# Another order table for the same 1,927 operations of a fused attention and gated MLP kernel

## The chip, the cores and the metric

One Trainium2 chip, one of its cores. The time is device microseconds of one execution of the whole program, as the median of several runs; lower is better. The engines are TensorE (PE, with PEld for its weight loads), VectorE (DVE), ScalarE (ACT), GpSimd (POOL) and SyncE (SP), which here issues every DMA.

## The reference

Causal attention over 4 batches, 12 heads, 448 positions and head size 64, then a gated MLP (768 wide, 1,024 inside) with a spatial gate, all in fp32:

```
scores = q @ k.T / sqrt(64); scores = where(causal, scores, -1e9)
attn   = softmax(scores); x = concat_heads(attn @ v)          # 4 x 448 x 768
h = gelu_tanh(x @ w_in); u, v = h[..., :512], h[..., 512:]
v_n = layernorm(v) * g_ln
v_s = einsum('ts,bsd->btd', w_sg, v_n) + b_sg
out = x + (u * v_s) @ w_out
```

## The kernel before

The 48 heads are worked as 24 pairs, p = 0 to 23, six to a batch; after a batch's six pairs comes its MLP. The five engines run far apart: pairs of the next batch are worked while PE does the MLP of the last.

**A pair.** q and k are loaded (L630, three buffers), PE makes the scores in two groups (L639, S0 and S1, in four PSUM banks with the tag s). DVE takes the row maxima with the mask (L653, eight a pair). ACT takes the exponentials into the P tiles and sums them (L661, ten a pair). DVE sums and inverts (L671, L672), PE transposes the inverses (L675, into one of the score banks), DVE copies them (L676), and two small DMAs and one large one spread them over the partitions (L680 rd, L683 rb). The exponentials must be transposed. For pairs 0 to 7 PE does it (L708, tags tx and ty), and ACT or DVE evict the result into a B buffer (L715, L713). For pairs 8 to 23 DVE does it with two stream transposes (L696, here called the first and the second turn of a pair), both into the one buffer A, which four DMAs copy into B (L700, `B<-P`). B has two slots. So the first turn of pair p writes A only when the four copies of pair p-1 have landed. Then PE multiplies by v (L738, PV, tag o; v is loaded at L732), DVE scales (L766), the result goes to DRAM (L771) and is split into a high and a low half on ACT or POOL (L774 to L779).

**The MLP.** `group` (L796) is every matmul of it, in operations of three: v (four groups of rows), u (four), s (the spatial gate, four), o (six). Each group takes a bank with the tag m. `gelu2` (L804 to L809) alternates ACT and DVE; layernorm is L847 to L864, the gate L908 to L914, the end L927 (residual load), L939 (add), L943 and L947 (stores).

**The weights.** w_in and w_out come in pieces through SP (L564), and each passes ACT (L566), DVE (L568, L570) and POOL (L573, L574). w_sg is L549 to L552, g_ln and b_sg L590 to L597.

**What sets the order.** Nothing runs as it is written. Every piece is added to an `Order` object with its engine, a duration that the planner assumes, what it reads and what it writes: 1,927 operations, of which 551 are PE's, 538 DVE's, 417 ACT's, 245 SP's and 176 POOL's. The table `ORDER` (from L92) gives each its rank: `ORDER[k] = n` makes operation n number k. `plan` takes, over and over, the engine that is free first in its own model and gives it the ready operation of lowest rank. The sequence that comes out is the program: each engine works its part strictly in that order. PSUM's eight banks and the buffers with several slots are handed out in the same sequence, so the order also sets whose bank an operation inherits, and whom it waits for.

Of the kernel before, what the change touches and what calls it, by code (L numbers as in the profile page):

```python
# [92 lines left out]
    1, 2, 84, 12, 4, 3, 118, 18, 5, 128, 6, 0, 172, 7, 24, 8, 162, 9, 10, 348, 85, 13, 14, 86, 15, 87, 16, 89, 11,  # L93
    88, 216, 17, 19, 90, 95, 91, 93, 96, 92, 129, 30, 94, 97, 20, 98, 99, 21, 130, 101, 133, 103, 22, 131, 100,
    134, 260, 23, 110, 102, 132, 25, 112, 104, 140, 26, 36, 105, 111, 27, 106, 139, 349, 28, 114, 113, 137, 29,
    141, 135, 115, 107, 116, 138, 108, 142, 173, 136, 146, 42, 117, 31, 32, 144, 33, 145, 119, 148, 175, 350, 34,
    177, 143, 176, 353, 35, 147, 178, 356, 183, 174, 149, 37, 109, 38, 185, 156, 48, 39, 184, 120, 304, 181, 157,
    40, 179, 150, 43, 154, 44, 186, 217, 41, 180, 351, 151, 155, 152, 160, 189, 45, 54, 354, 121, 182, 352, 187,
    218, 161, 357, 219, 188, 355, 221, 122, 359, 220, 158, 191, 192, 225, 206, 190, 222, 200, 46, 159, 634, 49, 50,
    47, 223, 163, 227, 193, 224, 153, 201, 164, 51, 231, 60, 165, 228, 123, 358, 204, 229, 226, 194, 124, 166, 230,  # L100
    205, 198, 233, 250, 52, 232, 261, 56, 234, 53, 195, 55, 196, 262, 263, 235, 265, 199, 57, 66, 236, 244, 360,
    678, 125, 264, 202, 245, 269, 58, 237, 203, 270, 361, 248, 271, 266, 238, 207, 278, 267, 273, 126, 167, 272,
    208, 268, 168, 276, 209, 62, 277, 210, 305, 59, 239, 294, 280, 249, 275, 197, 274, 242, 240, 309, 279, 169,
    307, 61, 458, 310, 72, 170, 243, 308, 475, 67, 281, 288, 63, 315, 246, 127, 289, 282, 68, 459, 247, 64, 283,
    598, 476, 316, 284, 69, 317, 306, 65, 318, 211, 241, 286, 313, 213, 212, 311, 292, 287, 314, 78, 635, 214, 312,
    722, 320, 293, 319, 290, 171, 639, 637, 70, 321, 477, 291, 74, 460, 322, 285, 71, 638, 324, 73, 251, 640, 323,
    75, 646, 252, 215, 325, 645, 253, 76, 254, 295, 648, 338, 255, 647, 77, 330, 79, 256, 332, 331, 80, 326, 636,
    257, 333, 327, 328, 81, 679, 764, 259, 641, 258, 643, 642, 296, 683, 681, 649, 297, 644, 82, 610, 298, 651,
    684, 334, 83, 668, 652, 299, 478, 650, 329, 682, 335, 461, 300, 301, 653, 654, 336, 302, 689, 655, 680, 337,
    690, 303, 691, 656, 806, 685, 662, 692, 657, 479, 687, 658, 663, 686, 462, 688, 695, 693, 660, 339, 696, 697,  # L110
    694, 340, 661, 341, 698, 342, 666, 699, 712, 343, 664, 659, 667, 700, 723, 345, 344, 665, 701, 702, 347, 346,
    724, 725, 727, 726, 362, 765, 728, 368, 733, 729, 463, 374, 734, 731, 767, 380, 769, 735, 480, 730, 848, 736,
    768, 464, 386, 492, 770, 481, 392, 493, 737, 465, 398, 363, 404, 706, 364, 466, 482, 494, 703, 707, 365, 467,
    495, 369, 366, 483, 367, 732, 509, 375, 376, 410, 381, 370, 468, 496, 741, 738, 371, 526, 377, 739, 372, 742,
    527, 382, 740, 373, 748, 393, 669, 387, 378, 416, 399, 379, 670, 405, 388, 422, 400, 671, 389, 749, 672, 390,
    510, 754, 391, 411, 511, 406, 394, 383, 497, 412, 417, 384, 673, 385, 528, 743, 674, 498, 424, 704, 407, 428,
    423, 395, 512, 434, 408, 484, 705, 409, 751, 744, 775, 529, 401, 750, 396, 469, 499, 530, 777, 402, 753, 397,
    745, 710, 500, 485, 746, 531, 403, 711, 501, 708, 440, 429, 470, 486, 766, 502, 446, 471, 709, 452, 418, 776,
    472, 752, 807, 425, 435, 419, 473, 1066, 426, 713, 413, 778, 420, 771, 811, 427, 714, 503, 773, 809, 474, 715,
    772, 747, 716, 487, 536, 774, 781, 796, 504, 779, 430, 537, 414, 717, 513, 421, 538, 810, 718, 783, 415, 780,  # L120
    514, 546, 782, 488, 431, 539, 784, 448, 505, 817, 489, 547, 432, 453, 548, 506, 819, 490, 433, 790, 549, 507,
    491, 556, 441, 447, 557, 675, 558, 454, 515, 508, 791, 719, 559, 540, 455, 794, 532, 677, 785, 541, 676, 516,
    795, 566, 533, 793, 517, 567, 721, 812, 534, 792, 720, 550, 518, 818, 551, 535, 542, 456, 568, 519, 457, 820,
    560, 543, 786, 520, 436, 561, 544, 521, 449, 522, 442, 808, 787, 450, 545, 788, 451, 755, 523, 1108, 815, 756,
    524, 813, 757, 816, 758, 525, 824, 797, 822, 838, 814, 798, 759, 789, 552, 799, 562, 443, 760, 553, 800, 761,
    444, 445, 563, 821, 569, 880, 437, 554, 574, 762, 570, 825, 582, 564, 555, 826, 575, 565, 438, 823, 439, 590,
    832, 571, 576, 591, 827, 763, 572, 833, 577, 592, 573, 828, 578, 849, 834, 801, 579, 835, 829, 850, 803, 851,
    836, 853, 852, 804, 580, 837, 1067, 857, 859, 855, 830, 854, 583, 581, 1150, 861, 1069, 858, 860, 593, 802,
    1070, 584, 805, 866, 856, 862, 585, 1077, 1071, 599, 586, 863, 604, 1072, 587, 865, 600, 594, 1079, 1078, 605,
    595, 867, 831, 1068, 1080, 874, 864, 588, 1109, 1192, 868, 1075, 589, 596, 1073, 839, 1076, 1074, 840, 597,  # L130
    1082, 1113, 841, 875, 1081, 842, 1084, 601, 1083, 1098, 869, 1086, 1111, 876, 1085, 606, 1114, 877, 1112, 870,
    602, 1120, 843, 879, 611, 1119, 1087, 878, 607, 871, 1122, 603, 845, 844, 616, 608, 1121, 872, 847, 617, 846,
    609, 1088, 1110, 1089, 1090, 1151, 1234, 1117, 1115, 1118, 1152, 1153, 1155, 1126, 1116, 1124, 618, 1276, 1154,
    1123, 1157, 619, 1128, 1159, 1127, 612, 873, 1156, 1125, 1092, 613, 614, 622, 1160, 623, 1161, 1091, 1093, 624,
    1163, 625, 615, 1096, 1168, 626, 1162, 1129, 1097, 628, 620, 1166, 1095, 1158, 1130, 629, 1164, 1131, 1170,
    1094, 630, 1165, 1132, 1167, 890, 1169, 621, 907, 1171, 627, 891, 1172, 892, 1173, 1174, 631, 1193, 632, 633,
    1194, 1195, 1197, 1196, 881, 1494, 1199, 1198, 882, 1133, 883, 1134, 884, 1099, 1140, 1200, 1203, 1100, 1030,
    1201, 1101, 1135, 1209, 1207, 1102, 1205, 908, 1182, 1211, 885, 1204, 1042, 1103, 909, 887, 1136, 1202, 1206,
    910, 1137, 888, 1210, 911, 1208, 1138, 889, 1212, 1139, 893, 1213, 886, 894, 1175, 1235, 1104, 1236, 1239,
    1237, 1240, 912, 1536, 1241, 1243, 924, 1238, 1244, 925, 1242, 1214, 895, 1215, 1216, 926, 896, 927, 913, 897,  # L140
    928, 914, 898, 929, 915, 1176, 941, 930, 899, 942, 1245, 1177, 1251, 943, 1247, 1249, 944, 931, 1181, 1250,
    958, 900, 1253, 1180, 932, 968, 916, 1217, 1252, 959, 1246, 901, 933, 1178, 969, 1254, 917, 1179, 1248, 960,
    934, 978, 918, 1255, 961, 919, 902, 920, 962, 903, 921, 979, 904, 980, 935, 905, 936, 970, 937, 922, 906, 988,
    963, 1105, 938, 1141, 945, 923, 1218, 1142, 939, 1143, 1144, 946, 1106, 1183, 1224, 1219, 947, 1184, 1107,
    1185, 940, 948, 1186, 1220, 971, 1145, 1222, 949, 1187, 964, 972, 1266, 950, 1221, 973, 965, 1223, 998, 974,
    951, 1146, 989, 966, 975, 1188, 990, 952, 1147, 967, 991, 976, 953, 1149, 1189, 954, 992, 977, 1148, 999, 981,
    955, 982, 1190, 956, 993, 957, 1006, 1191, 1260, 983, 1007, 984, 1261, 1008, 994, 1000, 985, 1014, 1265, 995,
    1001, 986, 1264, 1009, 996, 1002, 1262, 1015, 987, 1003, 1263, 1016, 997, 1017, 1010, 1022, 1004, 1018, 1011,
    1256, 1277, 1257, 1258, 1005, 1012, 1278, 1279, 1281, 1280, 1495, 1578, 1013, 1282, 1287, 1285, 1225, 1288,
    1283, 1019, 1499, 1226, 1259, 1497, 1289, 1286, 1227, 1290, 1500, 1294, 1228, 1284, 1292, 1267, 1308, 1498,  # L150
    1506, 1268, 1229, 1269, 1291, 1230, 1293, 1270, 1295, 1496, 1508, 1526, 1302, 1296, 1020, 1537, 1231, 1620,
# [854 lines left out]
```

## Time and profile before

| | |
|---|---|
| median of 3 runs | 354.4 us (353.96 to 354.82) |
| the profiled execution's own time | 355.62 us |
| its span, first to last instruction | 353.8 us |
| mean granted TensorE clock | 0.998 |
| PE busy | 339.1 us, 96% of the span |
| PE's weight loads (PEld) | 269.2 us, 76% |
| DVE, ACT, POOL busy | 260.0 us (73%), 196.6 us (56%), 149.9 us (42%) |
| data moved | 69.50 MB, mean 196 GB/s |

A busy share is a mean over stages. PE stands still for some 15 us in all, so the places where it does are few and can be looked at one by one. Times inside the program are counted from the start of the span. The profiled execution is 1.2 us longer than the median of the runs.

### The profile page before, as it was taken

The numbers are of one execution on the slowest core, as the hardware profiler recorded it, in microseconds if no ns is written. First come the engines' busy times: TensorE is split into PE (matmuls) and PEld (weight loads), VectorE is DVE, ScalarE is ACT, GpSimd is POOL, SyncE is SP. The second block draws the span as 40 slices with busy tenths as digits, with TensorE's granted clock in tenths as the row PEclk, the third lists the DMA queues.
The fourth block names the chain that finished last, engine by engine and source line by source line (L and its number), as shares of the span: only waits on it lengthen the run. The fifth ranks groups of instructions, "written<-read, shape, count | busy, mean of one in ns | idle before, by whom it ended". The sixth has DMA issues, their size and how long they took to land.

```text
span 353.8 us, 6879 instructions
## 1 busy us (share of the span) xinstructions
PE 339.1 (96%) x2231; PEld 269.2 (76%) x2231; DVE 260.0 (73%) x762; ACT 196.6 (56%) x658; POOL 149.9 (42%) x200
## 2 busy tenths in 40 slices
PE   7698999989999999999999999998999999999995
PEld 3455667657888778776898888776898898889995
DVE  2999978689999988756899987377897721258613
ACT  2999987777856957237443885218344700135410
POOL 4567887236977720010653641001265700242550
PEclk9999999999999999999999999999999999999999
DMA  7988987697855887797575786889465455400004
GB/s 237 374 284 292 304 287 228 196 287 210 248 123 173 219 238 250 242 298 248 151 173 128 235 236 176 269 240 295 121 200 126 139 119 196 155 2 1 0 2 156
DMA packets 37972, 69.50 MB, mean 196 GB/s; under 512 B 3888, under 2 KB 18992, under 8 KB 37936
## 3 DMA queue, kind: packets, MB, share of 16 engines
q1 hardware_dynamic: 37936, 69.06, 64.2%
q8 instruction: 18, 0.29, 0.3%
q14 instruction: 18, 0.15, 0.1%
HBM read 39.68 MB, written 12.58 MB: 148 GB/s over the span
## 4 chain that ended last, share of the span: by engine, by line
PE 69%; DMA 13%; DVE 9%; ACT 4%; SPq 3%; issue 1%; POOL 1%; DVEq 0%; POOLq 0%
PE m L796 47%; PE o L738 10%; PE s L639 8%; DMA B<-P 5%; ACT P L661 3%; DVE s L653 3%; DVE P L696 2%; DMA vn<-in_w_in_dram 2%; DMA out_dram<-res 2%; DMA rb<-rd 2%; PE tx L708 1%; DMA g<-in_w_out_dram 1%; DMA res<-xd 1%; PE ty L708 1%; SPq L680 1%
## 5 line engine op out<-in xcount | busy, mean ns | idle before, releaser
L661 ACT ACTIVATE P<-s,ngm 64x64 f32<-64x64 f32 (+3 forms) x240 | 100.3, 432 | 38.6 <-DVE ngm L653 18.4
L653 DVE CUSTOM_DVE_ANT_0 s<-s,mask 128x192 f32<-128x192 f32 (+3 forms) x192 | 75.3, 444 | 5.8 <-PE s L639 5.8
L796 PE MATMUL m<-win,x 128*128 128x512 f32 (+1 forms) x264 | 67.1, 399 | 0.0
L796 PE MATMUL m<-x,win 128*128 128x448 f32 x288 | 64.1, 370 | 1.8 <-ACT P L661 1.1
L796 PE MATMUL m<-g,wout 128*128 128x448 f32 x288 | 62.1, 368 | 0.0
L796 PEld LDWEIGHTS m<-x,win 128*128 128x128 f32 x288 | 53.3, 188 | 8.4 <-ACT P L661 1.9
L796 PEld LDWEIGHTS m<-g,wout 128*128 128x128 f32 x288 | 53.4, 188 | 5.4 <-issue 0.2
L796 PEld LDWEIGHTS m<-win,x 128*128 128x128 f32 (+1 forms) x264 | 46.8, 183 | 12.5 <-ACT P L661 0.6
L639 PE MATMUL s<-qk 64*128 64x448 f32 (+3 forms) x384 | 53.5, 403 | 1.8 <-DMA qk<-in_qk_dram 1.7
L639 PEld LDWEIGHTS s<-qk 64*128 64x128 f32 (+1 forms) x384 | 33.6, 178 | 23.2 <-issue 13.2
L661 ACT ACTIVATION_READ_ACCUMULATOR P<-s,ngm 128x1 f32 (+1 forms) x240 | 49.6, 207 | 0.0
L738 PE MATMUL o<-B,vraw 128*64 128x64 f32 (+4 forms) x672 | 47.2, 292 | 2.0 <-ACT P L661 1.4
L777 POOL TENSOR_TENSOR x<-xt,x 128x448 fp32r<-128x448 f32 x24 | 27.8, 1162 | 46.1 <-ACT x L776 45.9
L696 DVE STREAM_TRANSPOSE P<-P 128x1024 f32<-128x1024 f32 x32 | 39.3, 1233 | 9.5 <-DMA B<-P 4.4
L738 PEld LDWEIGHTS o<-B,vraw 128*64 128x64 f32 x672 | 33.0, 137 | 15.9 <-issue 6.3
L796 PE MATMUL m<-wsg,vn 128*128 128x448 f32 x176 | 39.6, 369 | 0.0
L851 POOL TENSOR_TENSOR mv<-mv,mhalf 128x1 f32<-128x1 f32 (+1 forms) x16 | 9.4, 592 | 67.7 <-DVE mv L849 67.2
L796 PEld LDWEIGHTS m<-wsg,vn 128*128 128x128 f32 x176 | 32.7, 188 | 3.2 <-issue 0.2
L804 ACT ACTIVATE tmp<-m 128x448 f32<-128x448 f32 (+1 forms) x28 | 15.2, 565 | 22.7 <-PE m L796 21.1
L807 ACT ACTIVATE tmp<-tmp 128x448 f32<-128x448 f32 (+2 forms) x32 | 18.9, 603 | 14.4 <-DVE tmp L805 14.1
L653 DVE DVE_READ_ACCUMULATOR2_ANT ngm<- 128x1 f32 (+1 forms) x192 | 25.7, 134 | 0.0
L805 DVE SCALAR_TENSOR_TENSOR tmp<-tmp,m 128x448 f32<-128x448 f32 (+1 forms) x28 | 17.3, 633 | 11.2 <-ACT tmp L804 11.1
(77 smaller groups left out, 379.5 us busy)
## 6 DMA issues: line engine op xcount, KB each, us to landing
B<-P SPq DMA_DIRECT2D x64, 256.0 KB
qk<-in_qk_dram SPq DMA_DIRECT2D x24, 448.0 KB
vn<-in_w_in_dram SPq DMA_DIRECT2D x12, 512.0 KB
vraw<-in_vP_dram SPq DMA_DIRECT2D x24, 256.0 KB
rb<-rd SPq DMA_DIRECT2D x24, 256.0 KB
xd<-xt SPq DMA_DIRECT2D x24, 224.0 KB
res<-xd SPq DMA_DIRECT2D x9, 448.0 KB
out_dram<-res SPq DMA_DIRECT2D x9, 448.0 KB
```

What stands on the lines that cost most here:

```text
L639: nc.tensor.matmul(out=s[z][bk].t[0:w, col:col + n], lhsT=qk_.t.rearrange("p a s -> p (a s)")[r, q0:q0 + w], rhs=qk_.t[r, 1, 0:n], start=T ...
L653: nc.vector.tensor_tensor_reduce(out=o, in0=o, in1=mk, scale=-0.125, scalar=3e38, op0=ALU.add, op1=ALU.min, accum_out=ngm[ib[z]][c][0:m])
L661: act(n, lambda c=c, m=m, k0=k0, n=n, bk=bk, col=col, off=off, kc=kc, i=i, z=z: nc.scalar.activation(out=P[i][0:m, off:off + n], in_=s[z][ ...
L696: dve(PW, lambda z=z: nc.vector.transpose(A[ia][:, :, :, z, :].rearrange("p g t k -> p t g k"), P[ib[z]]), Pk[z] + [kp], Ak, Tt, 1.105)
L708: nc.tensor.transpose(out, P[ib[z]][:, col:col + 128], ident)
L738: nc.tensor.matmul(out=dst(o.t[r]), lhsT=vr.t[:, c, r], rhs=src(z), start=first and n == 0, stop=last and n == len(lst) - 1)
L777: pool_tt(S, lambda: nc.gpsimd.tensor_tensor(out=y.t[:, S + 64:], in0=x.t, in1=f(y.t)[:, 0:S], op=ALU.subtract), [x, y], [(y, 1)], Ty)
L796: nc.tensor.matmul(out=ps.t[0:l().shape[1], 0:n], lhsT=l(), rhs=rr(), start=(k == 0), stop=(k == len(mms) - 1))
L804: act(n, lambda: nc.scalar.activation(out=z(), in_=h(), func=AF.Square), [ps], [t], at)
L805: dve(n, lambda: nc.vector.scalar_tensor_tensor(out=z(), in0=z(), scalar=1.0 / GC, in1=h(), op0=ALU.add, op1=ALU.mult), [ps], [t], at)
L807: act(n, lambda: nc.scalar.activation(out=z(), in_=z(), func=AF.Tanh, scale=GS * GC), [], [t], at, True)
L851: od.add("pool", 0.46, lambda mv=mv, m=m: nc.gpsimd.tensor_tensor(out=mv.t[0:m, 1:2], in0=mv.t[0:m, 1:2], in1=mhalf[0:m], op=ALU.pow), ["s ...
```

## The change

Only the table `ORDER` is another. The operations, their number, shapes, buffers, slots and the planner are the same. The new table was searched with an objective of which three quarters take transfers to land late. Its first rows:

```
 ORDER = (
-    1, 2, 84, 12, 4, 3, 118, 18, 5, 128, 6, 0, 172, 7, 24, 8, 162, 9, 10, 348, 85, 13, 14, 86, 15, 87, 16, 89, 11,
...
+    2, 4, 84, 1, 12, 5, 18, 6, 3, 24, 7, 128, 8, 0, 172, 9, 118, 10, 162, 11, 348, 85, 13, 14, 86, 87, 89, 15, 19,
...
```

Three places show what it moves.

**DVE in the head of the program, around the first pair's inverse.** `vn` is a piece of w_in on its way through L568 and L570; ngm_101 to ngm_108 are row maxima of pair 1; `tot` and `rs` are the sum and the inverse of pair 0. Before:

```order
L653 ISA s,ngm_105<-s,mask 64x64
...
L653 ISA s,ngm_104<-s,mask 128x448
L653 ISA ngm_104 128x1
L568 TENSOR_SCALAR vn<-vn 128x512
L671 TENSOR_REDUCE tot<-sm_117 128x8
L672 RECIPROCAL rs<-tot 128x8
L570 SCALAR_TENSOR_TENSOR vn<-vn 128x512
```

and in the change:

```order
L568 TENSOR_SCALAR vn<-vn 128x512 x2
L570 SCALAR_TENSOR_TENSOR vn<-vn 128x512 x2
L653 ISA s,ngm_105<-s,mask 64x64
...
L653 ISA s,ngm_104<-s,mask 128x448
L653 ISA ngm_104 128x1
L671 TENSOR_REDUCE tot<-sm_117 128x8
L672 RECIPROCAL rs<-tot 128x8
```

Two w_in pieces, not one, now pass whole ahead of pair 1's maxima and of the inverse; before, the second stood around the inverse. In the same stretch SP issues two more w_in loads ahead of pair 1's q and k, and the first v load behind them. On PE all seven warming matmuls (L538) come ahead of pair 0's scores, where one of them stood behind.

**SP where w_out is loaded, at pair 7.** `g` is a piece of w_out, `rd_127<-rT_123` the inverses of pair 7. Before:

```order
L680 DMA rd_127<-rT_123 4x16x128 x2
L564 DMA g<-in_w_out_dram 128x384 x4
L630 DMA qk<-in_qk_dram 128x896
L564 DMA g<-in_w_out_dram 128x384 x4
L683 DMA rb<-rd_127 128x1x512
L564 DMA g<-in_w_out_dram 128x384 x3
```

and in the change:

```order
L630 DMA qk<-in_qk_dram 128x896
L564 DMA g<-in_w_out_dram 128x384 x7
L680 DMA rd_127<-rT_123 4x16x128 x2
L564 DMA g<-in_w_out_dram 128x384 x2
L683 DMA rb<-rd_127 128x1x512
```

Seven of the sixteen w_out pieces now stand ahead of the DMAs that wait for pair 7's inverses; before, all stood behind.

**DVE around pair 20's first turn.** `P_92<-P_90` is a turn of pair 20; ngm_101 to ngm_108 are row maxima of pair 21, ngm_93 to ngm_100 of pair 22. Before:

```order
L653 ISA s,ngm_106<-s,mask_83 128x192
L653 ISA ngm_106 128x1
L848 BN_AGGR mv<-st 128x2
L696 STREAM_TRANSPOSE P_92<-P_90 128x8x4x32
L849 TENSOR_SCALAR mv<-mv 128x1
L653 ISA s,ngm_103<-s,mask 128x320
L653 ISA ngm_103 128x1
L653 ISA s,ngm_98<-s,mask_83 128x192
```

and in the change:

```order
L653 ISA s,ngm_103<-s,mask 128x320
L653 ISA ngm_103 128x1
L653 ISA s,ngm_93<-s,mask 64x64
L653 ISA ngm_93 64x1
L653 ISA s,ngm_107<-s,mask 128x320
...
L848 BN_AGGR mv<-st 128x2
L696 STREAM_TRANSPOSE P_92<-P_90 128x8x4x32
L653 ISA s,ngm_96<-s,mask 128x448
L653 ISA ngm_96 128x1
```

The last maxima of pair 21 and the first two of pair 22 are moved ahead of the turn.

## Rows read from the trace of the kernel before

**Rows 1.** The page, busy time: us (share of the span) xinstructions.
```profile
PE 339.1 (96%) x2231; PEld 269.2 (76%) x2231; DVE 260.0 (73%) x762; ACT 196.6 (56%) x658; POOL 149.9 (42%) x200
```

**Rows 2.** Waits of PE: line <- releaser: us in total, times, longest.
```profile
PE s L675 <- DVE rs L672: 2.0, 1, 2.0
PE s L639 <- DMA qk<-in_qk_dram: 1.7, 1, 1.7
PE o L738 <- ACT P L661: 1.4, 1, 1.4
PE m L796 <- ACT P L661: 1.1, 1, 1.1
...
PE m L796 <- DVE tmp L809: 0.6, 1, 0.6
```

**Rows 3.** Windows in the head: stretch, length, PE, PEld, DVE, ACT, POOL, clock, DMA, GB/s.
```profile
8.00:10.20 2.20, 0.53 (x5) 0.10 (x1) 2.20 (x12) 1.15 (x3) 1.63 (x2) 1.00 1.01 402
...
26.00:38.00 12.00, 10.42 (x82) 6.83 (x80) 11.83 (x46) 11.91 (x44) 9.63 (x11) 1.00 0.89 309
```

**Rows 4.** The page's costliest group of DVE: forms xcount | busy, mean ns | idle before.
```profile
L653 DVE CUSTOM_DVE_ANT_0 s<-s,mask 128x192 f32<-128x192 f32 (+3 forms) x192 | 75.3, 444 | 5.8 <-PE s L639 5.8
```

**Rows 5.** Timeline of PE in the head: start, us, engine, line, operation [idle before].
```profile
4.79 3.41 PE L639 MATMUL s<-qk 64*128 64x448 f32 x16
...
10.22 2.06 PE L639 MATMUL s<-qk 64*128 64x448 f32 x16 [1.70 <-DMA qk<-in_qk_dram]
...
15.35 0.27 PE L675 MATMUL s<-ident,rs 128*8 128x128 f32 x1 [2.04 <-DVE rs L672]
```

**Rows 6.** The chain that ended last, in the head: start, us, what.
```profile
15.20 0.56 DVE vn L570
```

**Rows 7.** The same chain at pair 6's PV.
```profile
67.62 0.28 SPq L680
...
71.02 5.10 DMA g<-in_w_out_dram
...
76.52 1.15 ACT P L661 x6
77.72 1.96 PE o L738 x20
```

**Rows 8.** The same chain from pair 14's first turn to its PV.
```profile
156.16 7.00 DMA B<-P
163.29 1.25 DVE P L696
164.53 0.58 DVE tmp L809
165.16 8.38 PE m L796 x39
173.54 3.68 PE o L738 x64
```

**Rows 9.** The same chain at pair 20's first turn.
```profile
231.83 4.74 DMA B<-P
236.69 1.25 DVE P L696
...
244.78 2.18 PE m L796 x9
```

**Rows 10.** Timeline of DVE: second turns of pairs 11, 13, 17, 19; first of 18.
```profile
124.14 1.23 DVE L696 STREAM_TRANSPOSE P<-P 128x1024 f32<-128x1024 f32 x1
...
149.02 1.24 DVE L696 STREAM_TRANSPOSE P<-P 128x1024 f32<-128x1024 f32 x1
...
201.15 1.24 DVE L696 STREAM_TRANSPOSE P<-P 128x1024 f32<-128x1024 f32 x1
...
210.19 1.25 DVE L696 STREAM_TRANSPOSE P<-P 128x1024 f32<-128x1024 f32 x1 [0.20 <-DMA B<-P]
...
224.20 2.37 DVE L696 STREAM_TRANSPOSE P<-P 128x1024 f32<-128x1024 f32 x2 [1.85 <-DMA vraw<-in_vP_dram]
```

192 rows, old and new, of the table ORDER are left out of this document.

## The prediction

> **What bounds the kernel now.** I read the page's busy times first. PE works 339.1 of 353.8 us [rows 1]; the reader is to see that only the 14.7 us in which PE stands can be won by an order, because the change takes no instruction away. Part of it lies ahead of the first matmul and behind the last one. Next come the waits of PE, for the rest [rows 2]. Two lie in the head: 1.7 us on pair 1's q and k, 2.0 us on pair 0's inverse. Three lie later, one wait each: 1.4, 1.1 and 0.6 us. The windows of the head show why PE does not recover there: from 26 to 38 us it works 10.42 of 12 us while DVE works 11.83 and ACT 11.91 [rows 3]. So up to some 38 us DVE and ACT bound the kernel, and from there PE does, but for the three waits. The chain that ended last, read at these three places, tells where each comes from.
>
> - Pair 6's PV, 77.72. SP stood for pair 7's inverses until 67.62, the w_out pieces queued behind them; the piece issued at 71.02 landed 5.10 us later; ACT, which works in order, stood for it, did its step and only then, at 76.52, six exponentials of pair 8 [rows 7]. PV had inherited a score bank of pair 8.
> - Pair 14's first turn. The copies out of A landed 7.00 us after 156.16, the turn ran, and only then the L809 that frees a bank for the matmul at 165.16 [rows 8].
> - Pair 20's first turn. The copies issued at 231.83 landed 4.74 us later, and behind the turn stood the maxima of pairs 21 and 22 that the bank of the matmul at 244.78 waited for [rows 9].
>
> **The change part by part.** It removes and adds no instruction, so everything is position; PE's changes of tile shape number 81 in either order, hence nothing there.
>
> *The head.* With each operation at its duration in the trace (DVE's largest group is L653, 444 ns, [rows 4]) I added up, at each operation that PE waits for, what the other engine has to do until then, less what PE has to do. The largest excess is how far PE must fall behind. DVE: 6.0 us before (at pair 4's L675), 4.8 in the change. ACT: 4.9 before (at pair 2's PV), 4.2 in the change. That is a gain of 0.7 to 1.2; I take 1.0. The bounds: two w_in loads are issued ahead of pair 1's q and k and the first v load behind them, a net 256 KB, which at the 402 GB/s of that stretch [rows 3] delays these scores (at 10.22, [rows 5]) by 0.65 us; and one L570 of 0.56 us [rows 6] moves ahead of pair 0's inverse. Exposed in full they cost 1.2 with no gain. At the other end both waits of the head, 3.7 us together, could shrink by half, 2. I stay near the middle because DVE's work fills the time until q and k land.
>
> *Pair 6's PV.* Seven w_out pieces are issued ahead of the wait for pair 7's inverses, some 4 us of PE's work earlier, and by the banks that the new order hands out this PV follows its own eviction, not pair 8's exponentials. That eviction has 7.0 us of ACT's work ahead of it and 8.3 us of PE's: 1.3 us to spare. Gain 1.4. What is late next is that eviction; a late w_out piece in front of it could still cost up to the 1.4 again.
>
> *Pair 14's first turn.* In the change the matmul that needs a bank at this place waits for the copy L676 of pair 15, which comes directly behind the turn and has some 2 us to spare, so a wait as long as the one seen hides. Gain 0.6, at least 0.
>
> *Pair 20's first turn.* The last maxima of pair 21 and two of pair 22 stand ahead of the turn, and the bank at this place comes from a v group of the MLP. Gain 1.1, at least 0.
>
> *The tail.* The change ends with one split add and one other, as before with two; nothing, within 0.5.
>
> *New waits.* The A chain has less room in places, below. Nothing shows its cost; the bounds are 0 and the rival's 3.6. The two waits at turns that rows show cost 0.6 and 1.1 [rows 2]; I take one such, 0.9.
>
> Sum: -1.0 - 1.4 - 0.6 - 1.1 + 0.9 = -3.2. Against the profiled execution's 355.62 that is 352.4; the median of the runs, 354.4, stands 1.2 below it, so 351.2.
>
> **The rivals.**
>
> *A, slower: the A chain.* Each pair from 8 on needs A empty, and DVE stands at the first turn until the copies of the pair before have landed. From the end of a second turn to that landing, where DVE waited for it: 7.8 us from pair 17 to 18, 13.0 from 13 to 14, 10.1 from 19 to 20 [rows 8 to 10]. In the change less DVE work fills this time: 4.7 us ahead of pair 18 (6.6 before), 4.9 ahead of pair 19 (6.4). So DVE stands more, and PE pays where what follows has no room. The place that decides is pair 14's PV, four such links behind pair 11's second turn. In the trace of before 48.2 us lie between them (124.14 + 1.23 to 173.54, [rows 8, 10]); PE's work between them in the change is 45.4, of which three double turns with what is between them take 7.8: 37.6 us for four links, 9.4 each. Up to 9.4 nothing happens, and without new waits the sum gives 351.2 - 0.9 = 350.3. At 10.3, the mean of the three seen, it costs 4 x 0.9 = 3.6 and gives 353.9, no change. At 11 it costs 6.4 and gives 356.7, slower. It decides at 10.6 (4 x 1.2 = 4.8, and 355.1). For it speaks the 13.0. Against it: the three seen are those that DVE had to wait for, so the long ones, and before PE did not wait at this PV with 2.8 us more of room.
>
> *B, part of the gain: the head gives nothing.* If q and k and the L570 are exposed, the head costs 1.2 instead of winning 1.0: 351.2 + 2.2 = 353.4. The clock belongs here. In the trace PE stood 1.70 us ahead of 10.22 and the granted clock of that stretch was 1.00 [rows 3, 5]; the sixteen score matmuls of pair 0 before it took 3.41 us, those of pair 1 2.06. With all warming matmuls ahead and q and k later the gap would be some 2.7 us. If the clock fell to its lower level, 1.2 GHz, pair 1's scores would cost 3.41 - 2.06 = 1.35 us more and end 352.6, hidden in part under DVE's work. The Trainium skill, "TensorE: Matmul & The Clock Gate", Part 1, has the rule that speaks against this change: an array that stands idle falls back to half its rate and must earn the full one again. The trace shows no fall at the 1.70 us gap, so it neither bears the rule out nor refutes it for a longer one.
>
> *C, no change: waits change places.* With PE at 96% each stage hands its delay on; if three new waits like the old ones (1.4, 1.1, 0.6) come up and the head gives 0.5, the sum is -0.5: 353.9. For it speaks that several places in the new order have under 0.8 us to spare by the same sums: the last add of batch 0 behind pair 11's turns, pair 22's transposed inverse ahead of pair 23's, pair 19's copies, which wait for pair 17's PV to free a B slot.
>
> *D, the change does nothing*: if the sequence came out the same. It does not: the engines' orders differ from the first rows.
>
> On the price of a copy out of A the rows alone decide: 4.74 and 7.00 us [rows 8, 9]. The Trainium skill, "SBUF — State Buffer", The DMA setup-cost knee, gives a fit of 2 us plus the bytes over 436 GB/s; an estimate by that page is 2.6 us for 256 KB. By it rival A would be dead; the trace disagrees, so A keeps its chance.
>
> **How the numbers follow.** A measurement of this kernel can tell about 0.2%, 0.7 us, from no change. The forecast, with its new waits between 0 and 2, holds 0.58 (349.4 to 352.4); B 0.16 (352.4 to 353.7); C and A's mild form 0.12 (353.7 to 355.1); A's hard form 0.14 (above 355.1). Faster 0.74, same 0.12, slower 0.14. The low end of the range is all three waits gone, no new ones, and the head at 1.9: 354.4 - 3.1 - 1.9 = 349.4; the high end takes in C and part of A's mild form, 354.9. Some 0.05 is left below, 0.15 above.
>
> **What would show it.** Right: no wait of PE over 0.5 us at the places that stood at 77.72, 165.16 and 244.78; ACT without a wait of 1.7 us on w_out ahead of pair 6's PV; PE at pair 6's PV some 2 us earlier; DVE standing longer in sum at L696 for `B<-P`, yet PE's waits from 38 us on under 1.5 us in all. Wrong: PE waiting at a PV (L738) for `B<-P`, at pair 14 above all (A); pair 1's scores near 3.4 us, or L675 of pair 0 past 16 us without recovery (B); new waits of PE on ACT or DVE adding to 3 us (C).

## The result, and the profile after

The change takes 349.36 us (median of 4 runs, 348.67 to 350.23) against 354.42 of before: ratio 0.986, 95% interval 0.983 to 0.989. Forecast were 351.2 us and a gain of 3.2; measured is a gain of 5.1. The profiled execution took 349.76 us with a span of 347.9, so the two profiled executions lie 5.9 us apart, 0.8 more than the medians.

The page's busy times: PE has the work of [rows 1] in a span shorter by 5.9 us.

```profile
PE 338.4 (97%) x2231; PEld 269.2 (77%) x2231; DVE 259.1 (74%) x762; ACT 196.0 (56%) x658; POOL 150.0 (43%) x200
```

All waits of PE in the change (line <- releaser: us in total, times, longest):

```profile
PE s L639 <- DMA qk<-in_qk_dram: 2.8, 1, 2.8
PE m L538 <- DVE tmp L533: 1.5, 1, 1.5
PE m L796 <- ACT P L661: 0.5, 1, 0.5
PE tx L708 <- ACT P L661: 0.5, 1, 0.5
PE o L738 <- ACT B L715: 0.3, 1, 0.3
```

The three later waits of [rows 2] are gone; one new one of 0.5 us stands at 269.7. The wait on pair 0's inverse is gone too, that on pair 1's q and k grew from 1.7 to 2.8. The windows (stretch, length, busy time of PE, PEld, DVE, ACT, POOL, then clock, DMA share, GB/s) show two things: PE is full where it stood before, and the clock fell in the head.

```profile
10.00:13.00 3.00, 2.25 (x10) 1.34 (x12) 2.47 (x9) 3.00 (x16) 1.11 (x2) 0.61 1.03 366
13.00:16.00 3.00, 3.00 (x22) 2.19 (x20) 2.97 (x13) 2.52 (x11) 2.92 (x3) 0.82 0.88 309
66.00:80.00 14.00, 14.00 (x73) 11.29 (x73) 13.21 (x36) 11.49 (x33) 6.45 (x13) 1.00 0.70 227
150.00:166.00 16.00, 16.00 (x105) 12.46 (x104) 15.74 (x45) 10.31 (x33) 4.59 (x6) 1.00 0.89 273
236.00:246.00 10.00, 10.00 (x75) 8.34 (x72) 9.97 (x31) 6.96 (x24) 2.90 (x4) 1.00 0.54 127
246.00:300.00 54.00, 53.52 (x361) 45.89 (x360) 30.28 (x70) 18.45 (x54) 20.66 (x24) 1.00 0.61 168
```

PE's timeline in the head of the change, beside [rows 5]: after a gap of 2.84 us pair 1's scores take 3.67 us, where they took 2.06 behind a gap of 1.70. Ahead of pair 1's q and k SP issues three w_in loads in the change and two in before, so one more and not two; with the first v load moved behind them the net is the 256 KB that the forecast worked with.

```profile
4.55 3.36 PE L639 MATMUL s<-qk 64*128 64x448 f32 x16
10.75 3.67 PE L639 MATMUL s<-qk 64*128 64x448 f32 x16 [2.84 <-DMA qk<-in_qk_dram]
...
15.28 0.27 PE L675 MATMUL s<-ident,rs 128*8 128x128 f32 x1
```

**PE's lag.** The waits listed do not add up to the gain, so I worked out a second measure from the traces. For each PE operation: its start, less the sum of the durations of all operations ahead of it in PE's own order, each at the shorter of its two durations in the traces of before and of the change, idle time left out. What is left is what PE has lost up to there. The columns on the right are the experiments below; every column is the trace of one execution.

| PE work done, us | before | change | wout_loads | copies_first | cut_rev | cut_late | warm_again |
|---|---|---|---|---|---|---|---|
| 50 | 11.3 | 10.6 | 10.5 | 12.0 | 12.4 | 10.4 | 10.0 |
| 70 | 14.0 | 11.1 | 11.7 | 14.3 | 13.1 | 12.2 | 10.6 |
| 140 | 15.8 | 13.3 | 14.3 | 16.2 | 15.3 | 14.3 | 12.8 |
| 150 | 17.2 | 13.6 | 17.1 | 16.4 | 15.5 | 14.5 | 13.0 |
| 200 | 19.2 | 14.7 | 19.2 | 17.8 | 16.7 | 15.6 | 14.1 |
| 230 | 21.9 | 15.6 | 22.4 | 18.6 | 17.7 | 16.6 | 15.1 |
| 260 | 22.8 | 16.8 | 23.2 | 19.5 | 18.8 | 17.7 | 16.2 |
| 330 | 23.3 | 17.3 | 23.7 | 20.0 | 19.2 | 18.1 | 16.6 |

Against before, the change has won 0.7 us by 50 us of work, 2.9 by 70, 2.5 by 140, 3.7 by 150, 4.5 by 200, 6.3 by 230, 6.0 by 260 and 5.9 at the end.

The columns also show how far executions of one order lie apart. Up to some 47 us, before, wout_loads, copies_first, cut_rev and cut_late run the same operations in the same order; at 50 us of work they lie between 10.4 and 12.4. So a difference of under 2 us between two columns can be chance there. What is lost from 140 us of work to the end is steadier: some 7.4 us in before and 9.4 in wout_loads, which have the old order there, and 3.8 to 4.0 in the change, in cut_rev, cut_late and warm_again, and in copies_first.

### The profile page after: what moved, and what is told of

Read it like the earlier page. It is cut to its first block, busy times and chain, and to the rows that moved or that the text cites. A ratio compares the mean times of both kernels' runs of the same rounds, so it can differ in the third digit from the quotient of the medians.

```text
span 347.9 us, 6879 instructions
## 1 busy us (share of the span) xinstructions
PE 338.4 (97%) x2231; PEld 269.2 (77%) x2231; DVE 259.1 (74%) x762; ACT 196.0 (56%) x658; POOL 150.0 (43%) x200
## 4 chain that ended last, share of the span: by engine, by line
PE 85%; DVE 5%; ACT 5%; DMA 2%; issue 1%; SPq 0%; DVEq 0%
PE m L796 62%; PE s L639 10%; PE o L738 10%; ACT P L661 3%; DMA qk<-in_qk_dram 2%; DVE s L653 2%; PE tx L708 1%; PE ty L708 1%; DVE vn L568 1%; ACT vn L566 1%; DVE vn L570 1%; PE s L675 1%; ACT B L715 1%; DVE ngm L653 1%; ACT wsg L551 0%
## 5 line engine op out<-in xcount | busy, mean ns | idle before, releaser
L653 DVE CUSTOM_DVE_ANT_0 s<-s,mask 64x64 f32<-64x64 f32 (+3 forms) x192 | 75.5, 442 | 6.6 <-PE s L639 6.5
L796 PE MATMUL m<-x,win 128*128 128x448 f32 x288 | 63.3, 368 | 0.0
L796 PEld LDWEIGHTS m<-g,wout 128*128 128x128 f32 x288 | 53.4, 188 | 5.9 <-issue 0.2
L796 PEld LDWEIGHTS m<-win,x 128*128 128x128 f32 (+1 forms) x264 | 46.9, 183 | 12.2 <-issue 1.3
L639 PEld LDWEIGHTS s<-qk 64*128 64x128 f32 (+1 forms) x384 | 32.2, 183 | 24.0 <-issue 13.0
L738 PEld LDWEIGHTS o<-B,vraw 128*64 128x64 f32 x672 | 33.9, 137 | 15.6 <-issue 5.7
L796 PE MATMUL m<-wsg,vn 128*128 128x448 f32 x176 | 38.2, 367 | 0.5 <-ACT P L661 0.5
L776 ACT ACTIVATE x<-xt 128x448 fp32r<-128x448 f32 x18 | 10.4, 578 | 37.2 <-DVE xt L766 35.3
L912 POOL TENSOR_TENSOR tmp<-tmp,g 128x448 f32<-128x448 f32 x16 | 18.1, 1144 | 21.3 <-DVE tmp L908 21.2
L779 POOL TENSOR_TENSOR x<-xt,x 128x64 fp32r<-128x64 f32 x24 | 8.7, 362 | 40.8 <-ACT x L776 40.6
```

The costliest lines, as they stand in the source:

```text
L639: nc.tensor.matmul(out=s[z][bk].t[0:w, col:col + n], lhsT=qk_.t.rearrange("p a s -> p (a s)")[r, q0:q0 + w], rhs=qk_.t[r, 1, 0:n], start=T ...
L653: nc.vector.tensor_tensor_reduce(out=o, in0=o, in1=mk, scale=-0.125, scalar=3e38, op0=ALU.add, op1=ALU.min, accum_out=ngm[ib[z]][c][0:m])
L738: nc.tensor.matmul(out=dst(o.t[r]), lhsT=vr.t[:, c, r], rhs=src(z), start=first and n == 0, stop=last and n == len(lst) - 1)
L776: act(S, lambda: nc.scalar.activation(out=y.t[:, 0:S], in_=x.t, func=AF.Copy), [x], [y], Ty, True)
L779: pool_tt(64, lambda: nc.gpsimd.tensor_tensor(out=y.t[:, S:S + 64], in0=x.t[:, S - 64:], in1=f(y.t)[:, S - 64:S], op=ALU.subtract), [x, y] ...
L796: nc.tensor.matmul(out=ps.t[0:l().shape[1], 0:n], lhsT=l(), rhs=rr(), start=(k == 0), stop=(k == len(mms) - 1))
```

## The experiments

Two theories stood against each other. Theory 1, that of the forecast: each wait of PE is cured where it stood, and the gains add. Theory 2: behind 111 us the old order is held by the landing of the copies out of A, so what is won ahead of these places is lost again at them.

One expression is used in several kernels: the first K operations of one table's sequence, then the rest in the other's.

```
     def run(self):
-        for n in self.plan():
+        head, then = self.sequence(CHANGED)[:312], self.sequence(ORDER)
+        for n in head + [n for n in then if n not in set(head)]:
             self.ops[n]["fn"]()
```

Here `sequence(table)` ranks the operations by that table and returns `plan()`. CHANGED is the new table, ORDER the old one.

**The new head alone (cut_head), the edit above.** Expected:

> The first 312 operations (to about 47 us of PE's time) in the new sequence, the rest in the old one. By place (theory 1: each wait of PE is cured where it stood, and the gains add): the head is worth 0.9 us, so 353.5, with the waits of 1.4 us at pair 6's PV, 0.6 at a u matmul of batch 1 and 1.1 at one of batch 2 all still there. By handing on (theory 2: PE falls back on the next late operation, gains shrink behind the place): the gain of the head is eaten at pair 6's PV, which waits on an absolute time (the landing of a w_out piece): 354.2 to 354.6, with that wait grown to 2.3 us.

Measured: 355.02 us against 355.28 of before beside it, ratio 1.002 (0.998 to 1.006). The head alone is worth nothing that can be measured, as theory 2 has it in its result; theory 1's 0.9 us lies just outside the interval. In its detail neither is borne out: the wait at pair 6's PV did not grow to 2.3 us, it was absent, and three small ones of 1.5 us in all stood at transposes of other pairs, the two longest at 53.4 and 81.8 us (columns as above; the lines of the spliced kernels are 104 further down, L812 is L708). And PE's lag at 50 us of work is 11.6 here, 11.3 in before: in this execution the head had won no lead that could have been handed on.

```profile
PE tx L812 <- DVE xt L870: 1.5, 3, 0.7
...
PE m L900 <- ACT P L765: 1.1, 2, 0.7
```

**New up to 111 us (cut_wout): the same with 780 in place of 312.** Expected:

> The first 780 operations (to about 111 us) new, the rest old. Theory 1: head 0.9 plus pair 6's PV 1.7, so 351.8; the waits of 0.6 and 1.1 still there. Theory 2: 353.5 or more, since the A chain of pairs 11 to 14 sets its own time and the old order's wait behind pair 14's first turn grows from 0.6 by what was won.

Measured: 356.08, ratio 1.004 (1.000 to 1.007). The splice itself does harm: PE's lag, 11.5 at 100 us of work (before 14.9), is 15.6 at 120, since around pairs 10 to 13 the two orders differ in which operations have been done. It tells only that the lead was gone right behind the splice, not why; inconclusive between the theories.

**New up to 168 us (cut_b1): the same with 1112.** Expected:

> The first 1112 operations (to about 168 us) new, the rest old. Theory 1: 0.9 + 1.7 + 1.0 = 3.6, so 350.8, with one wait of 1.1 left behind pair 20's first turn. Theory 2: under 2.5 in all, with that wait grown past 2.

Measured: 352.8, ratio 0.995 (0.991 to 0.999), 2.5 us under before, with an interval from 0.4 to 3.1: at the bound of theory 2 and short of theory 1's 3.6. The wait behind pair 20's first turn is 1.1 us, as theory 1 had it, and did not grow past 2. The profiled execution, 354.64 us, was the longest of the ten. Its waits of PE show the place that the forecast's rival A had named, pair 14's PV:

```profile
PE o L842 <- DMA B<-P: 2.2, 2, 1.7
```

In the timeline this PV starts at 173.97, when the copies have landed. In the change it starts at 174.8, behind a second turn that ended 1.1 us sooner (165.6 against 166.7). There pair 15's first turn, which needs these copies landed, starts at 172.96:

```profile
172.96 1.25 DVE L696 STREAM_TRANSPOSE P<-P 128x1024 f32<-128x1024 f32 x1
```

So at rival A's place the change has at least 1.8 us of room.

**The old order with seven w_out loads moved (wout_loads).**

```
+        loads = [at["wout", c, j, 0] for c in range(2) for j in range(4)][:7]
+        seq = [n for n in seq if n not in loads]
+        k = seq.index(at["pair", 7, 24])
+        seq[k:k] = loads
```

`at` finds an operation by its name; ("pair", 7, 24) is the DMA of pair 7's inverses. Expected:

> The old order, and only seven w_out loads of SP moved ahead of the DMAs that wait for pair 7's inverses; bank and ACT order as before. If the place of the loads is the cause at pair 6's PV: the wait of ACT of 1.7 us on w_out and the wait of PE of 1.4 us go, 353.0. If the inherited bank of pair 8 is the cause and the load only its last link: PE still waits there, 0.5 us or more, 353.9. If the gain is handed on: the wait goes and 354.4 stays.

Measured: 354.32 against 355.28, ratio 0.999 (0.996 to 1.003). The wait of 1.4 us at pair 6's PV is gone with the bank as before. That alone does not show the place of the loads to be its cause, because the wait is not in every execution of the old order: it is 1.0 us in turn20, 0.5 in copies_first and absent in cut_late, whose order is the old one up to 111 us (lines 104 further down).

```profile
75.25 1.96 PE L842 MATMUL o<-B,vraw 128*64 128x448 f32 x20
```

The lag tells more. Between 60 and 70 us of work the five traces with the old order there (before, turn20, copies_first, cut_head, cut_late) lose 0.9 to 1.9 us, every one with the new order 0.3, and wout_loads 0.3 too. So in this one trace the place of the loads was enough, bank and ACT order as before. ACT's wait of 1.7 us on w_out did not go; it stands at 78.9, behind this PV.

But the time stays. PE's lag is 2.3 us less than before at 70 us of work (0.8 of it already at 50, where the order is the same), 1.5 at 140 and 0.1 at 150: all of it was lost at the matmul behind pair 14's first turn, where the wait of [rows 8] grew from 0.6 to 1.8 us (lines 5 further down).

```profile
PE m L801 <- DVE tmp L814: 1.8, 1, 1.8
```

That turn came at 162.9, and at 163.3 before; DVE stood 1.1 us longer for the copies. Here it is in this run, and then in before:

```profile
162.89 1.25 DVE L701 STREAM_TRANSPOSE P<-P 128x1024 f32<-128x1024 f32 x1 [3.46 <-DMA B<-P]
163.29 1.25 DVE L696 STREAM_TRANSPOSE P<-P 128x1024 f32<-128x1024 f32 x1 [2.32 <-DMA B<-P]
```

This is theory 2 at one place.

**The change once more (again).** No edit. Expected:

> The change itself beside the other runs, to see how far its executions lie apart. Theory 1 (waits cured, gains add): 1.4% under before, all executions within 1 us. Theory 2 (the old order is held at pairs 14, 16 and 20 by the landing of the copies out of A, and the new one stays clear of it): 1.4% under before, and executions in which PE waits at a PV for copies out of A are the long ones.

Measured: 349.71 (349.46 to 350.55), ratio 0.985 (0.979 to 0.991); before beside it 352.17 to 357.14. The executions of the change lie within 1.1 us, those of before within 5. Why before's lie so far apart is open: each kernel left the trace of one execution. The clock explains little of it. Of the 55 executions of before beside these runs, the ten with a mean granted clock of 1.000 took 354.3 us on the mean, the 21 with 0.995 took 355.1.

**The old head, the rest new (cut_rev): 312, with the two tables exchanged.** Expected:

> The first 312 operations (the head, to about 47 us) in the old sequence, the rest in the new one. Theory 1: the head's 0.9 us are lost: 0.9 above the change. Theory 2: behind the head nothing holds PE in the new order, so what the head loses is handed on to the end: 0.7 above the change, in the profile the same delay of PE behind 47 us to the end. Against both: if the new order is held by the copies as well, the loss is swallowed and the time is that of the change within 0.3.

Measured: 351.55 against 349.71 of the change on the same chip. PE's lag is 1.8 us above the change's at 50 us of work and 1.9 at the end: in the new order nothing behind the head swallows a loss. That refutes the swallowed loss; it does not part the two theories, which both let the loss reach the end. Nor is 1.8 us the price of the head: with the same old head before stands at 11.3 at 50 us of work, this run at 12.4, and cut_late, which keeps more of the old order, is faster.

**The old order up to 111 us, the rest new (cut_late): 780, exchanged.** Expected:

> The first 780 operations (to about 111 us) in the old sequence, the rest in the new one. Theory 1: the head's 0.9 and the 1.7 at pair 6 are lost, so 2.6 above the change and 2.5 below before. Theory 2: the gain sits in the part behind 111 us, where the old order was held: most of the 5 us stay, the rest 2 to 2.6 above the change as far as PE is the bound there; no wait of PE over 0.7 us at the old places (a u matmul of batch 1 at 165, pair 16's PV at 197, a u matmul of batch 2 at 245).

Measured: 350.68, ratio 0.988 (0.983 to 0.994), 1.0 above the change. Of some 5.2 us 4.2 stay: most of the gain sits behind 111 us, as theory 2 has it, and no wait of PE is left at the three old places there. The part ahead of 111 us is worth 1.0, where both theories had 2 to 2.6; in this execution the wait at pair 6's PV was absent.

**Warming matmuls in the gap (warm_gap, warm_again).** In the change the last of the seven is put behind pair 0's scores and issued twelve times:

```
+        last = at[11,]
+        seq.remove(last)
+        seq.insert(1 + seq.index(at["pair", 0, 2]), last)
+        for n in seq:
+            for _ in range(12 if n == last else 1):
+                self.ops[n]["fn"]()
```

> The change with twelve warming matmuls (L538) in the gap in which PE waits for pair 1's q and k, in place of the last of the seven ahead of it; nothing else. Pair 1's scores should then run at 2.4 GHz: 2.1 us, not 3.67. If the fall of the clock is hidden under DVE's work (pair 0's inverse is ready at 14.8, PE comes at 15.3): the time of the change within 0.4. If PE is the bound behind it: 1.4 below the change, 348.0.

> The change with the gap ahead of pair 1's scores filled by twelve warming matmuls, once more, since 349.19 against 349.71 did not tell them apart. If the clock kept up is worth what the profile showed (PE 0.8 us earlier from 20 us to the end): 1.7% under before, 0.983; if nothing: 0.985 or more.

Measured: 349.19 (4 runs) and 349.13 (6 runs), ratios 0.983 (0.978 to 0.988) and 0.982 (0.978 to 0.986), beside 349.36 and 349.71 of the change. All ten lie between 348.71 and 349.53, the eight of the change between 348.67 and 350.55. PE's timeline of warm_again, its lines 5 further down:

```profile
7.64 2.76 PE L543 MATMUL m<-tmp 128*128 128x512 bf16 x12
11.02 2.06 PE L644 MATMUL s<-qk 64*128 64x448 f32 x16 [0.62 <-DMA qk<-in_qk_dram]
...
14.51 0.27 PE L680 MATMUL s<-ident,rs 128*8 128x128 f32 x1 [0.40 <-DVE rs L677]
```

The scores are back at 2.06 us, and PE's lag is 0.5 to 0.7 less than the change's from 50 us of work to the end. So the fall of the clock was hidden in the greater part (it had cost 1.6 us at the scores), and the rest, about half a microsecond, is to be had. The two traces of the change point the same way: in the first the clock was down from 10.6 to 14.1 us, in again from 9.4 to 16.3, and again's span is only 0.3 us longer. This is the fastest version of the study, by less than its intervals tell apart.

**The old order with the copies out of A first on SP (copies_first).** The copies of each pair from 12 to 22 stand together; at pair 13 six loads go behind them:

```
+        for p in range(12, 23):
+            copies = [at["pair", p, i] for i in range(28, 32)]
+            a, b = min(map(seq.index, copies)), max(map(seq.index, copies))
+            late = [n for n in seq[a:b] if self.ops[n]["e"] == "sp" and n not in copies]
+            if p == 13:
+                late = [at[k] for k in (("pair", 18, 0), ("pair", 13, 25), ("pair", 13, 32),
+                                        ("o", 1, 0, 0), ("pair", 14, 32), ("o", 1, 2, 0))] + late
...
+            seq[k:k] = late
```

Expected:

> The old order; on SP alone the four copies out of A of each pair from 12 to 22 stand together, and six loads that stood ahead of pair 13's copies stand behind them. Nothing moves on another engine. If the old order is held behind 111 us by the landing of these copies (theory 2): the 13.0 us from pair 13's second turn to pair 14's first become about 8, the waits of PE at the u matmul of batch 1 (0.6) and at pair 16's PV go, that of batch 2 shrinks, and the time falls by 1 to 3 us. If what was cured in the new order is the place of the turns among DVE's work and the banks (theory 1): the time of before within 0.7.

Measured: 351.56 against 355.12, ratio 0.988 (0.983 to 0.994): 3.6 us, from SP's order alone. SP's timeline in before, where q and k of pair 18, one rb load, two residual loads and two v loads stand ahead of pair 13's copies though its second turn had ended at 150.3:

```profile
149.38 1.10 SPq L630 DMA_DIRECT2D qk<-in_qk_dram  x1
150.58 0.72 SPq L683 DMA_DIRECT2D rb<-rd  x1
151.35 0.58 SPq L732 DMA_DIRECT2D vraw<-in_vP_dram  x1
...
153.56 3.46 SPq L700 DMA_DIRECT2D B<-P  x4
```

and in copies_first (lines 12 further down):

```profile
151.03 3.41 SPq L712 DMA_DIRECT2D B<-P  x4
154.48 1.06 SPq L642 DMA_DIRECT2D qk<-in_qk_dram  x1
```

From pair 13's second turn to pair 14's first it now takes 10.2 us, not 13.0 [rows 8, 10]; 8 were expected. DVE does not stand for the copies at that turn, so the 10.2 are its own order, and the copies landed sooner than that. Over all turns its wait for them falls from 4.4 us to 1.2:

```profile
DVE P L708 <- DMA B<-P: 1.2, 2, 0.6
```

The waits at the u matmuls of batches 1 and 2 are gone; the one at pair 16's PV, 0.15 us in before, is 0.12. PE's lag is above that of before up to 140 us of work and 3.3 us below it at the end. That the copies out of A held the old order behind 140 us is shown by this: nothing moved on PE, DVE, ACT or POOL. The change has the same cure at pair 13: its copies are issued from 154.58 on, when the second turn has ended at 154.55; in before 3.3 us lie between.

**The copies of pairs 11 to 13 twice, in the change (copies_twice).**

```
+        copies = [at["pair", p, i] for p in (11, 12, 13) for i in range(28, 32)]
+        for n in seq:
+            for _ in range(2 if n in copies else 1):
+                self.ops[n]["fn"]()
```

> The change, with the four copies out of A of pairs 11, 12 and 13 each issued twice (the same bytes to the same place). Each link grows by some 2.4 us of issue and the transfer of 1 MB more. If the new order's room at pair 14's PV is as narrow as the forecast's rival had it (9.4 us a link): PE waits there for the copies, 2 to 6 us, and the time rises by as much. If the room is wide: within 0.7 of the change, some 349.7 where before is 354.9.

Measured: 395.05 us, 45 more. The edit did not do what it was for: a second copy to the same place waits on SP for the first to have landed, as the eight of pair 11 show,

```profile
129.85 20.36 SPq L703 DMA_DIRECT2D B<-P  x8
```

so everything behind them on SP stood. It says nothing of the room at pair 14's PV. It gives a price. The single issues are

```profile
129.85 0.60 SPq L703 DMA_DIRECT2D B<-P  x1
135.37 1.20 SPq L703 DMA_DIRECT2D B<-P  x2
140.10 1.19 SPq L703 DMA_DIRECT2D B<-P  x2
144.47 1.19 SPq L703 DMA_DIRECT2D B<-P  x2
149.67 0.54 SPq L703 DMA_DIRECT2D B<-P  x1
```

where a line with x2 is the second copy of one quarter of B and, 0.6 us later, the first of the next. From a first copy's issue to that of its second, which waits for its landing, it is 5.5 us for the first quarter, which came right behind other loads, and 4.1, 3.8 and 4.6 for the others, each with one more copy under way. For pairs 12 and 13 it is 6.9 and 5.7, then 3.7 to 4.2.

**Pair 20's first turn moved on DVE, in the old order (turn20).**

```
+        turn = at["pair", 20, 26]
+        seq.remove(turn)
+        seq.insert(seq.index(at["pair", 20, 27]), turn)
```

> The old order; pair 20's first turn alone is moved on DVE behind the three maxima that stood between its two turns. The forecast's account of the wait of 1.1 us in batch 2 had two parts. If the maxima behind the turn made it: the wait goes, 1.1 below before. If it was the bank of pair 22, whose exponentials cannot start until pair 20's tiles are read by both turns: the wait stays at 1.1 within 0.3 and the time that of before.

Measured: 354.08 against 355.12, ratio 0.997 (0.993 to 1.000). In its profile the wait of 1.1 us is gone, which stands in every other trace with the old order at this place but copies_first (1.1 in cut_wout, cut_b1 and wout_loads, 0.7 in cut_head); both turns run together from 237.46 for 2.36 us and end at 239.8, where the second ended at 240.6 before. The first of the two stands in [rows 9].

```profile
237.00 0.54 DVE L857 TENSOR_SCALAR tmp<-tmp,mv 128x512 f32<-128x512 f32 x1
237.46 2.36 DVE L700 STREAM_TRANSPOSE P<-P 128x1024 f32<-128x1024 f32 x2
```

So it was the maxima, and that the old order handed pair 22's bank on would not by itself have cost the 1.1. The median falls by 1.0, but the interval reaches 1.000, so that the gain reaches the end is likely and not shown.

## Why the prediction was right, and where it was off

The measured time, 349.36, lies at the low edge of the range (349.4); the sign, the places and the signs of the terms were right, the size was not: 5.1 won where 3.2 were forecast. That it falls on the edge is in part luck. The edge was worked out as no new wait and a head worth 1.9, and neither came: what lies beyond the forecast was won behind 111 us, where it had the smaller part. Of the 3.2 it put 2.4 ahead of 111 us and 0.8 behind it; cut_late has 1.0 ahead and 4.2 behind, the lag of the two first traces 2.5 up to 140 us of work and 3.4 behind. By its own steps, with PE's lag as the measure:

- **The head**, forecast 1.0: 0.7 by 50 us of work, 1.2 by 60, in two traces, which is less than executions of one order differ by. Over six traces with the new head the lag at 50 is 9.8 to 11.6, on the mean 10.7; over six with the old one 10.4 to 12.4, on the mean 11.5. So the head is worth some 0.8, and the excess of DVE's and ACT's work gave the right size. That the seven warming matmuls start 0.7 us sooner (1.45, not 2.12) gave nothing: by 10 us of work the two lags are level within 0.3.
- **Pair 6's PV**, forecast 1.4 for two reasons: 1.7 between 60 and 70 us of work. Of the two reasons the place of the loads is enough, as far as one trace shows (wout_loads). Read as one wait the term would have been unsafe: in four traces of the old order this wait is 1.4, 1.0, 0.5 and 0. PE comes to this PV at 80.54, not sooner, since other work of PE now stands ahead of it; by the lag it is 2.9 ahead at 70 us of work. Between 70 and 140, 0.4 are handed back.
- **Pair 14's first turn**, forecast 0.6: 1.1 between 140 and 150. **Pair 20's first turn**, forecast 1.1: 1.8 between 200 and 230. In between 0.9, around pairs 16 and 18, for which there was no term.
- **New waits**, forecast 0.9: 0.8 between 250 and 260, at one place, the s matmul at 269.7.
- **The tail**, forecast nothing: nothing.

The step that was mis-sized is "Three lie later, one wait each: 1.4, 1.1 and 0.6 us". I took the list of PE's waits for the whole price. From 140 us of work to the end before lost 7.4 us and the change 4.0; the waits that a list shows there come to 1.9 and 0.5. The rest, 2.0 of 3.4, lies inside operations. The two largest make 1.1 of it: before, the first score group of pair 18 took 1.44 us where it takes 0.87 in the change, the second one of pair 22 1.47 where it takes 0.97, and the profile counts PE as busy, since the next weights wait and the end of a matmul is modelled. PE's weight loads show the idle time of the first of them in before (start, us, engine, line [idle before <- releaser]):

```profile
193.82 0.62 PEld L639 LDWEIGHTS s<-qk 64*128 64x128 f32 x5 [0.29 <-DVE tmp L908]
194.68 0.14 PEld L639 LDWEIGHTS s<-qk 64*66 64x66 f32 x1 [0.24 <-issue]
```

The sum's form was wrong as well, and the figure did not suffer for it. The forecast added terms as if each could be had alone. In the old order they cannot: the head alone gave nothing that could be measured, and what the loads alone won was lost at pair 14's first turn, which kept the landing time of its copies. For the head no trace shows where a gain would have gone. That the gains add in the change because it loosens these places too fits cut_late and copies_first; it is not shown term by term.

The rivals: A (the A chain) named the mechanism that held the old order, but put it on the wrong side. I expected DVE to stand longer at the turns. It stood 4.4 us in all before,

```profile
DVE P L696 <- DMA B<-P: 4.4, 4, 2.3
```

and less in the change,

```profile
DVE P L696 <- DMA B<-P: 2.9, 3, 1.5
```

and pair 14's PV was clear. The four links from pair 11's second turn to the landing of pair 14's copies took at most 10.8, 9.1, 8.5 and 7.4 us in the change, 8.9 on the mean, under the rival's 9.4. B's clock came true: the gap grew to 2.84 us and the granted clock of the next stretches was 0.61 and 0.82. It cost 1.6 us at the scores (1.35 in the forecast), of which about half a microsecond reached the end. C (waits change places) is what happens when a part of the change is made alone.

## What to carry to other kernels

Before you add up cured waits, ask of each later place whether PE or a transfer sets its time; a place that is set by a landing swallows whatever was won ahead of it, and is to be cured first. In a queue that issues in order, put the copies on which an in-order engine stands ahead of loads that are wanted later. Measure by PE's lag behind its own work: the list of waits showed 1.4 of the 3.4 us that were won behind 140 us and left out the rest. And before one wait in one trace is called a cause, look for it in other executions of the same order.

## What was not expected of the hardware

- A gap of 1.70 us ahead of pair 1's scores left the granted clock at 1.00, one of 2.84 us took it down to 1.2 GHz (0.61 and 0.82 of full speed over the next stretches, 3.67 us for work of 2.06). Ahead of both stood pair 0's sixteen score matmuls and seven warming ones, one of the seven directly ahead of the gap in before. The Trainium skill, "TensorE: Matmul & The Clock Gate", Part 1, says that an array left idle goes back to half its rate; the change agrees, and behind the gap of before no fall shows. The length of the gap alone does not place the fall: in copies_first, with a gap of 2.99 us, it came at 11.6 us, inside these scores (2.53 us); in cut_late, with 2.77, the scores took 2.06 and the clock fell at 15.5 us, behind the 2.05 us in which PE stood for pair 0's inverse.
- Copies of 256 KB out of A into B took 3.7 to 4.6 us from issue to landing with one other such copy under way, and 5.5 to 6.9 with other loads beside them (copies_twice). The Trainium skill, "SBUF — State Buffer", The DMA setup-cost knee, has a fit by which an estimate for 256 KB is 2.6 us; every copy seen here and in [rows 8, 9] took longer, and no run has one alone.
- One order of the same operations can be steadier than another: the executions of before beside these runs lie between 351.9 and 357.6 us, those of the change between 348.7 and 350.6. It goes with the part behind 111 us: cut_rev and cut_late, new there, lie within 1.2 and 1.4 us (four executions each), cut_head and wout_loads, old there, within 5.0 (ten each). That the landings make the difference is argued, not shown; copies_first, four executions, still spreads over 2.6.
